# Head sums of two token groups moved from TensorE matmuls to a gather and VectorE additions, with the work around them re-ordered

## The chip, the cores and the metric

The kernel runs on one core of one Trainium2 chip. The metric is device time in microseconds (us). A run is compared with runs of the kernel before on the same chip. "PE" is TensorE's matmul side, "PEld" its weight loads, "DVE" VectorE, "ACT" ScalarE, "POOL" GpSimd, "SP" the engine that issues most loads.

## The reference, cut to what matters

Two layers; in each, dilated local attention (32 heads of 32, window of 8 positions with stride 2) and then a gelu feed-forward, each with layer norm and residual. S = 2048, D = 1024, F = 3584, bfloat16.

```python
x = A_x                                    # (1, 2048, 1024)
for _ in range(2):
    x = x + attention(layernorm(x))        # q, k, v = x @ wqkv; logits[s, w] = q[s] . k[s - 2w] * scale
                                           # masked where s - 2w < 0; softmax over w; values; @ wo
    x = x + gelu(layernorm(x) @ w1 + b1) @ w2 + b2
```

## The kernel before

Tokens go in groups of 512: groups 0 to 3 are the first layer, 4 to 7 the second. Per group: `gen_qkv` (192 full matmuls), `gen_wo` (the output projection, 64), `gen_ffn1` and `gen_ffn2` (224 each). The attention's products and sums are VectorE's, run beside the matmuls of other groups as "sides" of a stage. A group's softmax weights `a` are then spread, that is, copied by DMA to all partitions that need them (`abc`), and the products with V give the attention values `oT`, which the output projection reads. For a group's logits, products of Q and K chunks are added up over eight chunks (`new_prod`), and what is left must be summed over the four partitions of each head. Groups 2 and later do that by a DMA gather and three VectorE additions; groups 0 and 1 by matmuls with a 0/1 selector, in `head_sum`:

```python
def acc_tile():
    return psum.tile([P, T], F32, name="acc", bufs=6)          # six PSUM banks; "L" has the two others
...
def head_sum(n, last=True):
    ...
    for wh in range(2):
        for tb in range(NTT):                                  # four column tiles of the array
            mm(L[tb * H:(tb + 1) * H, wh * 4:(wh + 1) * 4, :], lhsT=smat[:],
               rhs=prod[:, tb, wh * 4:(wh + 1) * 4, :], start=start, ..., tile_position=(0, tb * H))
...
def ln_stats_ahead(g):                                         # group 3's statistics, on VectorE
    for tt in range(NTT):
        ln_stats(g * NTT + tt, mv_ahead[:, tt, :], rstd_ahead[:, tt, :])
...
# gen_qkv, group 0: four quarters of the weights as they land, on half the tokens
for kq in range(4 if n == 0 else 0):
    for c in range(6):
        first[c] = qkv_chunk(wq, c, xnT, first.get(c), kq * (KD // 4), (kq + 1) * (KD // 4), 0, 2)
        if (kq, c) in ((2, 5), (3, 5)):
            ...
            transpose_on_pe(*first_late.pop(0))                # tiles 2 and 3
...
# the main program
stage(q1, sides=at(6, attend, 0) + at(6, spread, 0) + at(6, hold) + each(new_prod, 1, 8, 1, 0, 4) + each(av, 0, 12, 1))
q2 = gen_qkv(2, defer=True)
stage(q2, 18)
new_prod(1, 4)
hold()
stage(gen_wo(0))                                               # reads oT, which av(0, c) writes
```

PSUM is the memory into which matmuls add up their results; each accumulation takes one bank of it. A bank of `acc` comes free when its reader has read it: for `gen_ffn2` and `gen_wo` that reader is VectorE. In the traces it takes its instructions one after the other in a fixed order, so such a read, here called a clear, can come late because other work stands ahead of it (4.4 us late in one place shown below).

## Time and profile before

| | before |
|---|---|
| median of the first 3 runs | 1233.41 us |
| span of the profiled run | 1230.8 us |
| PE busy, DVE busy | 99%, 70% |
| first real matmul; first of full width; last matmul | 8.92; 24.39; 1227.46 us |
| start to start of full matmuls | 0.216 us |

From the page of the kernel before, its part 1 (busy us, share of the span, instructions) and part 2 (granted TensorE clock in 40 slices):

```profile
PE 1222.2 (99%) x5739; PEld 632.6 (51%) x5789; DVE 861.9 (70%) x922; ACT 307.3 (25%) x491; POOL 87.2 (7%) x207
PEclk9999999999999999999999999999999999999999
```

From the list of waits of the kernel before, PE alone (engine, what it wanted, whom it waited for: total us, times, longest):

```profile
PE acc L219 <- DVE xn L93: 1.5, 1, 1.5
PE acc L118 <- DVE big L93: 1.1, 1, 1.1
PE acc L118 <- DMA wt<-in_A_wqkv_dram: 0.3, 1, 0.3
```

PE waits 2.9 us in all, and all of that lies before 12.1 us. Busy time alone would not show saturation, as matmuls overlap (one lasts 0.379 us in the trace); the starts do: after 24 us those of full matmuls are 0.216 us apart, but for a few longer steps around the two head sums (and steps of 0.43 us where the record of a matmul is missing). So only the two ends and whatever else PE has to do are to be gained.

Timeline of PE around the first head sum, kernel before (start us, us, engine, line, operation, output<-inputs, count):

```profile
62.80 1.46 PE L118 MATMUL acc<-xnT,wt 128*128 128x512 bf16 x6
64.19 0.61 PE L118 MATMUL L<-big,smat 128*32 128x512 bf16 x8
64.74 1.52 PE L118 MATMUL acc<-xnT,wt 128*128 128x512 bf16 x6
```

The eight selector matmuls start within 0.24 us (64.19 to 64.43), four at a time: four column tiles run side by side. From the first of them to the next full matmul it is 0.55 us.

Timeline of VectorE before the first output projection, and at the first clears of the first and second feed-forward, kernel before:

```profile
84.68 4.62 DVE L93 TENSOR_TENSOR big<-big 128x4096 bf16<-128x4096 bf16 x2
89.22 4.49 DVE L93 TENSOR_TENSOR big<-abc,vT 128x4096 bf16<-128x4096 bf16 x2
...
122.75 0.75 DVE L93 TENSOR_TENSOR oT<-big 128x512 bf16<-128x512 bf16 x2
...
222.19 0.67 DVE L93 TENSOR_TENSOR tmp<-acc,b2bc 128x512 f32<-128x512 f32 x1
...
371.65 0.69 DVE L93 TENSOR_TENSOR tmp<-acc,b2bc 128x512 f32<-128x512 f32 x1
```

Group 0's values begin at 89.22 us and end at 123.50; the projection starts at 125.23. The lines with `tmp<-acc` free PSUM banks.

### The profile page before, as it was taken

What the parts mean: (1) busy time and instruction counts of PE and PEld (TensorE: products, weight loads), DVE (VectorE), ACT (ScalarE), POOL (GpSimd) and SP (SyncE); (2) the same over time, 40 slices, a digit from 0 to 9 for tenths busy, and PEclk for the clock granted to TensorE, in tenths of its full rate; (3) what the DMA queues carried; (4) which work ended last, traced back from release to release, by engine and by line L of the source; (5) the groups of instructions that cost most, each with busy time, mean ns of one, the idle gap of its engine ahead of it and who ended that gap; (6) DMA issues with size and microseconds to landing.
All of it is one profiled execution on the core that took longest, in us unless ns stands there. A gap on an engine that the chain in (4) does not pass through costs nothing.

```text
span 1230.8 us, 13962 instructions
## 1 busy us (share of the span) xinstructions
PE 1222.2 (99%) x5739; PEld 632.6 (51%) x5789; DVE 861.9 (70%) x922; ACT 307.3 (25%) x491; POOL 87.2 (7%) x207
## 2 busy tenths in 40 slices
PE   9999999999999999999999999999999999999998
PEld 7666544456444564445544465444654444444444
DVE  7989899988998599375993759937599797011001
ACT  4343152014320143202431024310244101400310
POOL 3010010010010000100011000010000002000000
PEclk9999999999999999999999999999999999999999
DMA  9954665656556654856447565486664558446441
GB/s 290 300 179 143 182 222 185 201 154 209 181 165 215 180 162 163 229 172 186 150 163 238 171 171 170 158 223 202 171 196 145 188 196 208 151 158 196 155 135 52
DMA packets 219391, 225.06 MB, mean 183 GB/s; under 512 B 68194, under 2 KB 187136, under 8 KB 217024
## 3 DMA queue, kind: packets, MB, share of 16 engines
q1 hardware_dynamic: 214704, 208.69, 55.5%
q0 software_dynamic: 4624, 15.49, 3.3%
q8 instruction: 45, 0.74, 0.2%
q14 instruction: 18, 0.15, 0.0%
HBM read 191.11 MB, written 4.72 MB: 159 GB/s over the span
## 4 chain that ended last, share of the span: by engine, by line
PE 99%; DMA 1%; issue 0%; SPq 0%; DVE 0%
PE acc L118 98%; DMA wt<-in_A_wqkv_dram 1%; SPq L93 0%; PE L L118 0%; PE L L219 0%; DVE x L93 0%
## 5 line engine op out<-in xcount | busy, mean ns | idle before, releaser
L118 PE MATMUL acc<-xnT,wt 128*128 128x512 bf16 (+1 forms) x3392 | 720.9, 375 | 0.4 <-DMA wt<-in_A_wqkv_dram 0.3
L118 PEld LDWEIGHTS <-wt 128*128 128x128 bf16 x3392 | 400.5, 119 | 319.1 <-issue 1.4
L118 PE MATMUL acc<-wt,hT 128*128 128x512 bf16 (+1 forms) x1780 | 386.0, 376 | 2.1
L118 PEld LDWEIGHTS <-hT 128*128 128x128 bf16 x1820 | 178.1, 98 | 208.9
L93 DVE TENSOR_TENSOR big<-big 128x1024 bf16<-128x1024 bf16 (+2 forms) x184 | 245.2, 1360 | 2.2
L93 ACT ACTIVATE hT<-acc,b1T 128x512 bf16<-128x512 f32 x224 | 152.7, 688 | 332.3 <-PE acc L118 332.1
L93 DVE TENSOR_TENSOR big<-qT,kT 128x4096 bf16<-128x4096 bf16 x64 | 143.8, 2286 | 48.4 <-ACT kT L93 47.8
L93 DVE TENSOR_TENSOR big<-abc,vT 128x4096 bf16<-128x4096 bf16 x64 | 144.7, 2286 | 14.0 <-DMA abc<-a 13.4
L93 DVE TENSOR_TENSOR tmp<-acc,b2bc 128x512 f32<-128x512 f32 x56 | 38.6, 690 | 146.7 <-PE acc L118 143.7
L93 ACT CAST qT<-acc 128x512 bf16<-128x512 f32 (+1 forms) x72 | 38.0, 545 | 351.1 <-PE acc L118 351.1
L118 PE MATMUL acc<-wt,oT 128*128 128x512 bf16 x440 | 97.4, 379 | 0.4
L93 DVE BATCH_NORM_STATS2 stats<-x 128x6 f32<-128x512 bf16 x128 | 85.6, 682 | 4.5 <-DMA x<-in_A_x_dram 3.4
L118 PEld LDWEIGHTS <-oT 128*128 128x128 bf16 x448 | 43.8, 98 | 52.8
L93 DVE TENSOR_TENSOR x<-acc,big 128x512 bf16<-128x512 f32 (+1 forms) x9 | 5.7, 633 | 90.0 <-PE acc L118 90.0
L93 ACT CAST vT<-acc 128x512 bf16<-128x512 f32 x64 | 37.5, 586 | 83.3 <-PE acc L118 83.3
L93 ACT CAST kT<-acc 128x512 bf16<-128x512 f32 x64 | 37.4, 587 | 67.0 <-PE acc L118 67.0
L93 POOL TENSOR_TENSOR rstd<-mv,eps_t 128x1 f32<-128x1 f32 x56 | 14.2, 253 | 515.4 <-DVE mv L93 509.4
L93 DVE TENSOR_TENSOR x<-acc,x 128x512 bf16<-128x512 f32 x64 | 42.9, 671 | 4.8 <-PE acc L118 4.4
L93 DVE TENSOR_SCALAR xn<-x,mv,rstd 128x1024 bf16<-128x1024 bf16 x52 | 28.4, 547 | 20.2 <-POOL rstd L93 20.1
L93 DVE TENSOR_TENSOR x<-tmp,x 128x512 bf16<-128x512 f32 x56 | 38.7, 690 | 1.3
L93 POOL DMA_DIRECT2D big<-big x24 | 13.3, 565 | 256.3 <-DVE big L93 237.6
L93 POOL TENSOR_TENSOR rstd<-rstd,mhalf 128x1 f32<-128x1 f32 x56 | 31.0, 553 | 4.4
(68 smaller groups left out, 228.8 us busy)
## 6 DMA issues: line engine op xcount, KB each, us to landing
wt<-in_B_w_dram SPq DMA_DIRECT2D x56, 1024.0 KB, 5.7
wt<-in_B_w_dram SPq DMA_DIRECT2D x64, 896.0 KB, 4.9
wt<-in_A_wqkv_dram SPq DMA_DIRECT2D x46, 1024.0 KB, 5.6
wt<-in_A_wo_dram SPq DMA_DIRECT2D x16, 1024.0 KB, 5.0
big<-big POOLq DMA_DIRECT2D x24, 256.0 KB, 3.6
abc<-a POOLq DMA_DIRECT2D x24, 256.0 KB, 5.3
x<-in_A_x_dram SPq DMA_DIRECT2D x16, 256.0 KB, 6.2
out_dram<-x SPq DMA_DIRECT2D x31, 128.0 KB, 2.1
```

Of the source, the lines that this page charges most:

```text
L93: inst = f(*args, **kwargs)
L118: return pe(nc.tensor.matmul(*args, **kwargs))
```

## The change

Its intent: take the selector matmuls off PE, and make room on VectorE for what replaces them. Cut to its core:

```diff
-        return psum.tile([P, T], F32, name="acc", bufs=6)
+        return psum.tile([P, T], F32, name="acc", bufs=8)
...
-    def head_sum(n, last=True):  ...                      # gone; logits(n) sums a gather Lq for every group
+    def between(n, m):
+        vec.on = True                                     # VectorE in just this order
+        for c in range(3):
+            new_prod(m, c)
+        logits(n)
+        new_prod(m, 3, False)
+        weights(n)
+        spread(n)                                         # straight from SBUF; before: by way of DRAM
+        for _ in range(2):
+            add_prods(m)
+        vec.on = False
...
     def ln_stats_ahead(g):                                # group 3's statistics on ScalarE
+            act.activation(junk[:], x[t][:], ACT.Identity, scale=-1.0 / D, accum_out=less[:])
+            act.activation(junk[:], x[t][:], ACT.Square, bias=less[:], accum_out=var)
...
-            for c in range(6):
+            for c in range(7):
                 first[c] = qkv_chunk(...)
-                if (kq, c) in ((2, 5), (3, 5)):
+                if (kq, c) == (2, 3):  ...  transpose tile 2
+                if (kq, c) == (3, 4):  ...  transpose tile 3
...
-        hT = hpool.tile([P, KF, T], BF16, name="hT")
+        hT = [hpool.tile([P, KQ, T], BF16, name=f"hT{q}") for q in range(4)]
...
-        stage(q1, sides=at(6, attend, 0) + at(6, spread, 0) + at(6, hold) + each(new_prod, 1, 8, 1, 0, 4) + each(av, 0, 12, 1))
+        q1 = gen_qkv(1, defer=True, qk_pool=early, mix=NCH // 2)      # Q and K chunks take turns
+        stage(q1, sides=at(0, gather, 0) + at(11, between, 0, 1) + at(11, hold) + each(av, 0, 12, 1))
...
# group 2: products 4 to 7, its gather and softmax move from the first feed-forward
# to the V, Q and K chunks of group 3, after the second output projection
```

More of the change, by code (lines that the diff above doesn't have):

```diff
@@ L73 @@
     bigp = ctx.enter_context(tc.tile_pool(name="bigp", bufs=3))
-    dram = ctx.enter_context(tc.tile_pool(name="dram", bufs=2, space=bass.MemoryType.DRAM))
     smp = ctx.enter_context(tc.tile_pool(name="smp", bufs=1))
@@ L154 @@
     make_identity(nc, ident[:])
-    smat = const.tile([P, H], BF16, name="smat")
     mask = const.tile([P, W - 1, HALO], F32, name="mask")
@@ L166, in build_constants @@
         pool.memset(zhalo[:], 0.0)
-        pool.memset(smat[:], 1.0)
-        pool.affine_select(out=smat[:], in_=smat[:], pattern=[[-HP, H]], compare_op=ALU.is_ge, fill=0.0, base=0, channel_multiplier=1)
-        pool.affine_select(out=smat[:], in_=smat[:], pattern=[[HP, H]], compare_op=ALU.is_ge, fill=0.0, base=HP - 1, channel_multiplier=-1)
         pool.memset(mask[:], 0.0)
+        first = smp.tile([H, W - 1, HALO], F32, name="z")
+        pool.memset(first[:], 0.0)
         for w in range(W - 1):
-            pool.memset(mask[0:H, w, 0:HALO - DIL * w], -1e9)
-    def spread_mask():
-        first = smp.tile([H, W - 1, HALO], F32, name="mx")
-        vec.tensor_copy(first[:], mask[0:H, :, :])
-        vec.memset(mask[:], 0.0)
+            pool.memset(first[:, w, 0:HALO - DIL * w], -1e9)
         pool.dma_start(mask[0::NTT, :, :], first[:])
@@ L187, in transpose_bias @@
     def transpose_bias():
-        ps = psum.tile([P, KF], BF16, name="acc", bufs=6)
+        ps = psum.tile([P, KF], BF16, name="acc", bufs=8)
         pe(nc.tensor.transpose(ps[:], b1_rows[:], ident[:KF, :KF]))
@@ L205, in ln_stats_ahead @@
     def ln_stats_ahead(g):
+        junk = lnp.tile([P, D], BF16, name="xn", bufs=3)
         for tt in range(NTT):
-            ln_stats(g * NTT + tt, mv_ahead[:, tt, :], rstd_ahead[:, tt, :])
+            t, mean, var = g * NTT + tt, mv_ahead[:, tt, 0:1], mv_ahead[:, tt, 1:2]
+            less = lnp.tile([P, 1], F32, name="less")
+            act.activation(junk[:], x[t][:], ACT.Identity, scale=-1.0 / D, accum_out=less[:])
+            act.activation(junk[:], x[t][:], ACT.Square, bias=less[:], accum_out=var)
+            pool.tensor_scalar(out=mean, in0=less[:], scalar1=-1.0, scalar2=None, op0=ALU.mult)
+            rstd = rstd_ahead[:, tt, :]
+            pool.tensor_scalar(out=rstd, in0=var, scalar1=1.0 / D, scalar2=EPS, op0=ALU.mult, op1=ALU.add)
+            pool.tensor_tensor(out=rstd, in0=rstd, in1=mhalf[:], op=ALU.pow)
     def ln_norm(t, mv, rstd, xn=None):
@@ L213, in ln_norm, with transpose_on_pe @@
         return xn
-    def transpose_on_pe(xn, out, pst=None, parts=None):
-        if pst is None:
-            pst = psum.tile([P, KD, P], BF16, name="acc", bufs=6)
+    def transpose_on_pe(xn, out, parts=None):
+        pst = psum.tile([P, KD, P], BF16, name="acc", bufs=8)
         for k in range(KD):
@@ L237, in ln_first @@
         vec.on = act.on = True
-        both = psum.tile([P, 2, KD, P], BF16, name="L", bufs=1)
         mvs = {}
@@ L267, in ln_first @@
         for tt in range(2, 4):
-            first_late.append((norm(tt), xa[0][:, tt, :, :], both[:, tt - 2, :, :]))
+            first_late.append((norm(tt), xa[0][:, tt, :, :]))
         vec.on = act.on = False
@@ L290, in qkv_chunk, with add_prods, new_prod @@
         return ps
-    def head_sum(n, last=True):
-        if "L" not in st[n]:
-            st[n]["L"] = psum.tile([P, W, P], F32, name="L", bufs=1)
-            start = True
-        else:
-            start = False
-        L = st[n]["L"]
-        prod = st[n]["prods"].pop(0)
-        for wh in range(2):
-            for tb in range(NTT):
-                mm(L[tb * H:(tb + 1) * H, wh * 4:(wh + 1) * 4, :], lhsT=smat[:],
-                   rhs=prod[:, tb, wh * 4:(wh + 1) * 4, :], start=start,
-                   stop=last, skip_group_check=True, tile_position=(0, tb * H))
-    def new_prod(n, c):
+    def add_prods(n):
+        tree = st[n]["prods"]
+        b = tree.pop()
+        vec.tensor_tensor(out=tree[-1][:], in0=tree[-1][:], in1=b[:], op=ALU.add)
+    def new_prod(n, c, add=True):
         s = st[n]
@@ L312, in new_prod, with gen_qkv @@
         vec.tensor_tensor(out=prod[:], in0=q.unsqueeze(2).to_broadcast([P, NTT, W, P]), in1=win_by_tile(s["kT"][:, c, :]), op=ALU.mult)
-        tree = s["prods"]
-        tree.append(prod)
-        if c % 2 == 1:
-            for _ in range(1 if c % (NCH // s["parts"]) == 1 else 2):
-                b = tree.pop()
-                vec.tensor_tensor(out=tree[-1][:], in0=tree[-1][:], in1=b[:], op=ALU.add)
-    def gen_qkv(n, parts=1, defer=False, qk_pool=None, v_late=False, qk_next=None):
+        s["prods"].append(prod)
+        if add and c % 2 == 1:
+            for _ in range(1 if c == 1 else 2):
+                add_prods(n)
+    def gen_qkv(n, defer=False, qk_pool=None, v_late=False, qk_next=None, v_first=False, mix=0):
         g = n % NG
@@ L323, in gen_qkv, with values @@
         s = st[n]
-        s["parts"] = parts
         s["prods"] = []
         qk_pool = qk_pool or attp
+        if v_first:
+            wv = load_qkv(2)
         wq = wq_first if n == 0 else load_qkv(0)
-        wk = load_qkv(1)
+        if not v_first:
+            wk = load_qkv(1)
+        def values():
+            vT = attp.tile([P, NCH, HALO + T], BF16, name="vT", bufs=2)
+            s["vT"] = vT
+            act.on = n > 2
+            act.copy(vT[:, :, 0:HALO], (zhalo if g == 0 else vhalo)[:])
+            act.on = False
+            for c in range(NCH):
+                ps = qkv_chunk(wv, c, xnT)
+                act.copy(vT[:, c, HALO:], ps[:])
+                yield
+            if g + 1 < NG:
+                act.copy(vhalo[:], vT[:, :, T:T + HALO])
+        if v_first:
+            yield from values()
+            wk = load_qkv(1)
         if n == 0:
@@ L339, in gen_qkv @@
         for kq in range(4 if n == 0 else 0):
-            for c in range(6):
+            for c in range(7):
                 first[c] = qkv_chunk(wq, c, xnT, first.get(c), kq * (KD // 4), (kq + 1) * (KD // 4), 0, 2)
-                if (kq, c) in ((2, 5), (3, 5)):
-                    for done in range(2 if kq == 3 else 0):
+                if (kq, c) == (2, 3):
+                    transpose_on_pe(*first_late.pop(0))
+                if (kq, c) == (3, 4):
+                    for done in range(2):
                         act.copy(qT[:, done, 0:2 * P], first[done][:, 0:2 * P])
                     transpose_on_pe(*first_late.pop(0))
+                    act.hold()
+        if n == 0:
+            first[7] = qkv_chunk(wq, 7, xnT, t0=0, t1=2)
         for c in list(first)[2:]:
             act.copy(qT[:, c, 0:2 * P], first[c][:, 0:2 * P])
-        for c in range(6 if n == 0 else NCH, NCH):
-            ps = qkv_chunk(wq, c, xnT, t0=0, t1=2)
-            act.copy(qT[:, c, 0:2 * P], ps[:, 0:2 * P])
-        for c in range(NCH):
-            t0 = 2 if n == 0 else 0
-            ps = qkv_chunk(wq, c, xnT, t0=t0)
-            act.copy(qT[:, c, t0 * P:], ps[:, t0 * P:])
-            yield
-        if n > 0 and not v_late:
-            wv = load_qkv(2)
         kT = qk_pool.tile([P, NCH, HALO + T], BF16, name="kT")
@@ L362, in gen_qkv, with query, key @@
         act.on = False
-        for c in range(NCH):
+        def query(c):
+            t0 = 2 if n == 0 else 0
+            ps = qkv_chunk(wq, c, xnT, t0=t0)
+            act.copy(qT[:, c, t0 * P:], ps[:, t0 * P:])
+        def key(c):
             ps = qkv_chunk(wk, c, xnT)
@@ L367, in gen_qkv @@
                 new_prod(n, c)
+        ahead = mix or NCH
+        turns = [(query, c) for c in range(ahead)]
+        for c in range(NCH):
+            turns.append((key, c))
+            if ahead + c < NCH:
+                turns.append((query, ahead + c))
+        for i, (chunk, c) in enumerate(turns):
+            if i == NCH and n > 0 and not v_late and not v_first:
+                wv = load_qkv(2)
+            chunk(c)
             yield
@@ L370, in gen_qkv @@
             act.copy(khalo[:], kT[:, :, T:T + HALO])
-        vT = attp.tile([P, NCH, HALO + T], BF16, name="vT", bufs=2)
-        s["vT"] = vT
-        if v_late:
-            wv = load_qkv(2)
-        act.on = n > 2
-        act.copy(vT[:, :, 0:HALO], (zhalo if g == 0 else vhalo)[:])
-        act.on = False
-        for c in range(NCH):
-            ps = qkv_chunk(wv, c, xnT)
-            act.copy(vT[:, c, HALO:], ps[:])
-            yield
-        if g + 1 < NG:
-            act.copy(vhalo[:], vT[:, :, T:T + HALO])
+        if not v_first:
+            if v_late:
+                wv = load_qkv(2)
+            yield from values()
     def gather(n):
@@ L388, in gather @@
         prod = s["prods"].pop(0)
-        Lq = bigp.tile([P, HP, W, P], BF16, name="big")
+        Lq = attp.tile([P, HP, W, P], BF16, name="abc") if n < 2 else bigp.tile([P, HP, W, P], BF16, name="big")
         s["Lq"] = Lq
@@ L400, in fold, with logits, weights @@
         return t[:, 0, :]
-    def attend(n):
+    def logits(n):
         s = st[n]
+        Lq = s.pop("Lq")
         e = smp.tile([P, W, P], F32, name="e")
-        if "Lq" in s:
-            Lq = s.pop("Lq")
-            vec.tensor_tensor(out=e[:], in0=Lq[:, 0, :, :], in1=Lq[:, 1, :, :], op=ALU.add)
-            for j in range(2, HP):
-                vec.tensor_tensor(out=e[:], in0=e[:], in1=Lq[:, j, :, :], op=ALU.add)
-            L = e
-        else:
-            head_sum(n)
-            L = s.pop("L")
-        if n % NG == 0:
-            p = H if n == 0 else P
-            vec.tensor_tensor(out=L[0:p, 0:W - 1, 0:HALO], in0=L[0:p, 0:W - 1, 0:HALO], in1=mask[0:p, :, :], op=ALU.add)
-        if n < 2:
-            mx = smp.tile([P, P], F32, name="mx")
-            vec.tensor_reduce(out=mx[:], in_=L[:].rearrange("p w t -> p t w"), axis=AX.X, op=ALU.max)
-            mx = mx[:]
-        else:
-            mx = fold(L, ALU.max)
-        vec.tensor_tensor(out=e[:], in0=L[:], in1=mx.unsqueeze(1).to_broadcast([P, W, P]), op=ALU.subtract)
+        vec.tensor_tensor(out=e[:], in0=Lq[:, 0, :, :], in1=Lq[:, 1, :, :], op=ALU.add)
+        for j in range(2, HP):
+            vec.tensor_tensor(out=e[:], in0=e[:], in1=Lq[:, j, :, :], op=ALU.add)
+        if n % NG == 0:
+            vec.tensor_tensor(out=e[:, 0:W - 1, 0:HALO], in0=e[:, 0:W - 1, 0:HALO], in1=mask[:], op=ALU.add)
+        mx = fold(e, ALU.max)
+        vec.tensor_tensor(out=e[:], in0=e[:], in1=mx.unsqueeze(1).to_broadcast([P, W, P]), op=ALU.subtract)
+        s["e"] = e
+    def weights(n):
+        s = st[n]
+        e = s.pop("e")
         act.on = 1 < n < N - 1
@@ L432, in attend @@
         s["a"] = a
+    def attend(n):
+        logits(n)
[4 more added lines that the diff above has]
+            new_prod(m, c)
+        logits(n)
+        new_prod(m, 3, False)
+        weights(n)
+        spread(n)
+        for _ in range(2):
+            add_prods(m)
+        vec.on = False
     def spread(n):
@@ L440, in spread @@
         s["oT"] = attp.tile([P, NCH, T], BF16, name="qT" if n == N - 1 else "oT")
-        if n < 2:
-            a_d = dram.tile([H, NTT, W, P], BF16, name="a_d")
-            for tb in range(NTT):
-                pool.dma_start(a_d[:, tb, :, :], a[tb * H:(tb + 1) * H, :, :])
-            a = a_d
         for j in range(HP):
@@ L494, in gen_ffn1 @@
                     mm(ps[:], lhsT=wt[:, k, jj * P:(jj + 1) * P], rhs=xnT[:, :, k, :], start=(k == 0), stop=(k == KD - 1))
-                act.activation(hT[:, j, :], ps[:], ACT.Gelu_apprx_tanh, bias=b1T[:, j:j + 1])
+                act.activation(hT[j // KQ][:, j % KQ, :], ps[:], ACT.Gelu_apprx_tanh, bias=b1T[:, j:j + 1])
                 yield
@@ L520, in gen_ffn2 @@
                         for k in range(KQ):
-                            mm(ps, lhsT=hT[:, kq * KQ + k, tt * P:(tt + 1) * P], rhs=wt[:, k, cs],
+                            mm(ps, lhsT=hT[kq][:, k, tt * P:(tt + 1) * P], rhs=wt[:, k, cs],
                                start=(kq == 0 and k == 0), stop=(kq == 3 and k == KQ - 1))
@@ L596 @@
         stage(gen_qkv(0, qk_next=early), sides=at(14, load_b2))
-        q1 = gen_qkv(1, defer=True, qk_pool=early)
-        stage(q1, sides=at(6, attend, 0) + at(6, spread, 0) + at(6, hold) + each(new_prod, 1, 8, 1, 0, 4) + each(av, 0, 12, 1))
+        q1 = gen_qkv(1, defer=True, qk_pool=early, mix=NCH // 2)
+        stage(q1, sides=at(0, gather, 0) + at(11, between, 0, 1) + at(11, hold) + each(av, 0, 12, 1))
         q2 = gen_qkv(2, defer=True)
         stage(q2, 18)
-        new_prod(1, 4)
         hold()
@@ L604 @@
         hold()
-        stage(q2, sides=each(new_prod, 1, 0, 1, 5, 8))
+        stage(q2, sides=each(new_prod, 1, 0, 1, 4, 8))
+        gather(1)
     hpool = ctx.enter_context(tc.tile_pool(name="hpool", bufs=1))
-    stage(gen_ffn1(0), sides=at(5, attend, 1) + at(5, spread, 1) + at(5, hold) + each(new_prod, 2, 2, 1)
-          + at(10, gather, 2) + at(10, hold) + each(av, 1, 10, 2, 0, 4))
+    stage(gen_ffn1(0), sides=each(new_prod, 2, 2, 1, 0, 3) + at(5, hold) + at(5, attend, 1) + at(5, spread, 1) + at(5, hold) + at(6, new_prod, 2, 3)
+          + at(10, hold) + each(av, 1, 10, 2, 0, 4))
     stage(gen_ffn2(0), sides=at(0, ln_stats_ahead, 3) + at(15, hold) + at(15, ln_a, 3, None, True) + each(av, 1, 16, 1, 4, 8) + at(23, hold))
     for n in range(1, N - 2):
-        stage(gen_wo(n), sides=at(0, spread, n + 1) if n > 1 else at(7, hold) + at(7, attend, 2))
-        stage(gen_qkv(n + 2), sides=(at(0, spread, 2) if n == 1 else []) + each(av, n + 1, 0, 2, 0, 3))
-        if n == 1:
-            spread_mask()
+        early_av = 3 if n > 1 else 0
+        stage(gen_wo(n), sides=(at(0, spread, n + 1) if n > 1 else []) + (at(7, hold) if n < 3 else []))
+        stage(gen_qkv(n + 2, v_first=n == 1), sides=each(av, n + 1, 0, 2, 0, early_av) if n > 1 else
+              each(new_prod, 2, 0, 1, 4, 8) + at(3, gather, 2) + at(10, hold) + at(10, logits, 2) + at(19, weights, 2) + at(19, spread, 2))
         gather(n + 2)
-        stage(gen_ffn1(n), sides=(at(20, attend, n + 2) if n + 3 == N else []) + each(av, n + 1, 8, 2, 3, 8))
+        stage(gen_ffn1(n), sides=(at(20, attend, n + 2) if n + 3 == N else []) + each(av, n + 1, 8 - 2 * (3 - early_av), 2, early_av, 8))
         if n + 3 < N:
```

## The prediction

> **What bounds it now.** TensorE. The page has PE busy 99% of 1230.8 us, clock 1.00, and the list of waits gives PE only 2.9 us of waiting, all before 12.1 us. Busy time alone would prove little (the Trainium skill, "Trainium Kernel Development and Optimization", Performance Expectations, calls it a bad metric because matmuls are pipelined), so I read start-to-start times in the timeline: 0.216 us for each 128x512 matmul from 24 us to the end; the 0.43 us steps are missing records. This agrees with "TensorE: Matmul & The Clock Gate", Part 1 (215.7 ns warm). The 5,632 full-width-equivalent matmuls need 5632 x 0.2158 = 1215.4 us, untouched by the change. Only about 15 us can be gained at all, mostly start (first real matmul at 8.92 us) and tail. VectorE is 70% busy, but 99% in 30 to 124 us.
>
> **What the change removes from PE.** Two head sums of 8 selector matmuls, at 64.2 and 159.9 us. From the last matmul before to the first after is 0.86 us, less its own 0.216: 0.64 us each, because the four column tiles overlap. Total 1.28 us. At the start, seven chunks instead of six per quarter give PE 0.44 us more work before the third weight piece, where it now stands 0.49 us; but the copy of tile 3's transpose then comes nearly due, so I count 0.35 us.
>
> **What it adds.** Group 0 and 1 logits go through a gather (about 5.4 us from first issue to last landing in group 2, hidden behind three products) and three VectorE additions (1.22 us each), 3.7 us a group, plus 0.2 us for fold instead of reduce. Layer statistics leave VectorE for ScalarE (6 us less in the first feed-forward stage), four products of group 2 move behind the second output projection: both relieve VectorE before 247 us, and use idle VectorE afterwards (over 20 us idle from 260 to 400 us). Quartered gelu buffer and eight PSUM buffers: PE did not wait there, so nothing.
>
> **The critical place.** Attention values of group 0 must be ready for the first output projection. Before: chain of VectorE from 29.7 us, values start 89.22, end 123.50; projection starts 125.23, its eighth matmul (which reads the last chunk) 126.7: slack 3.2 us. After: PE arrives about 1.0 us earlier (125.75 for that matmul). VectorE: 63.75 + three products and an addition 9.1 + logits 6.75 + product 2.3 + weights 3.65 = 85.7 (up to 0.5 more if exp is late); direct spread needs about 5.8 us as in group 2 (8.5 in group 3), so values start about 91.5, end about 125.9. I expect PE to wait 0 to 0.6 us there, perhaps 2 us if the spread meets weight loads. Later projections keep slack.
>
> **Sum.** 1233.4 - 1.28 - 0.35 + 0.3 = 1232.1 us. Range 1231.0 to 1234.5. Faster by over 2%: 1%; within 2%: 97%; slower by over 2%: 2%.
>
> **What would show it.** No selector matmuls, no 0.86 us steps; first full-width matmul at about 24.0 us instead of 24.39; VectorE waiting about 1 us for the spread near 90 us; PE in the list of waits with at most about 1 us for group 0's values near 125 us; all other steps still 0.216 us; VectorE busy time 4 to 6 us different, without effect.
>
> **What would make it wrong.** A slow spread or late exp makes the wait at 125 us 2 to 4 us; a static ScalarE or VectorE order that holds back PSUM evictions; the start losing more on the tile 3 transpose, which now shares the PSUM pool; group 2's later logits delaying the third projection.

## The result and the profile after

The changed kernel takes 1231.15 us (median of 6; 1230.84 to 1231.43) against 1233.31 us (median of 6; 1232.55 to 1233.82): ratio 0.9983, 95% interval 0.997 to 0.9996. The spans of the two profiled runs are 1229.1 and 1230.8 us. A gain is there, of 0.17%: far within 2%.

Part 1 of the page and the granted clock, kernel after:

```profile
PE 1221.3 (99%) x5723; PEld 632.7 (51%) x5773; DVE 864.2 (70%) x918; ACT 315.1 (26%) x507; POOL 105.2 (9%) x209
PEclk9999999999999999999999999999999999999999
```

PE alone and PEld alone in the list of waits, kernel after, the lines that matter:

```profile
PE acc L218 <- DVE xn L92: 1.1, 1, 1.1
PE acc L117 <- DVE big L92: 1.0, 1, 1.0
...
PEld L117 <- DVE oT L92: 0.3, 1, 0.3
```

The wait for the weights at the start is gone; one new wait, of 0.3 us, is put down to group 0's attention values (`oT`).

Timeline of PE where the head sum was, kernel after: one unbroken group.

```profile
61.64 5.56 PE L117 MATMUL acc<-xnT,wt 128*128 128x512 bf16 x25
```

Timeline of VectorE at the places shown of before, kernel after (in brackets the idle time before the line and what ended it):

```profile
84.06 4.61 DVE L92 TENSOR_TENSOR big<-big 128x4096 bf16<-128x4096 bf16 x2
90.65 4.50 DVE L92 TENSOR_TENSOR big<-abc,vT 128x4096 bf16<-128x4096 bf16 x2 [1.98 <-DMA abc<-a]
...
124.19 0.75 DVE L92 TENSOR_TENSOR oT<-big 128x512 bf16<-128x512 bf16 x2
...
216.57 0.69 DVE L92 TENSOR_TENSOR tmp<-acc,b2bc 128x512 f32<-128x512 f32 x1 [12.36 <-PE acc L117]
...
381.41 0.68 DVE L92 TENSOR_TENSOR tmp<-acc,b2bc 128x512 f32<-128x512 f32 x1
```

Three things are to be seen. The values end at 124.94 us, 1.4 us later than before, while PE comes about 1.2 us earlier. In the first feed-forward VectorE now waits for PE (12.36 us idle) instead of coming 4.4 us late. In the second it comes at 381.41 us for an accumulation that was ready at 368.1 us: 13.3 us late, where it had been 1.9 us late.

Where the time came from, by matmul starts in the traces ("first" is the first real matmul, "full" the first of full width, "last" the last one; all 14 traces):

```
                                    first    full-first   last-full   last-first
before                              8.919    15.468       1203.070    1218.538
after                               8.953    14.915       1201.915    1216.830
after, again (e11)                  9.039    14.914       1201.719    1216.633
e1 selectors five times             9.424    14.915       1207.357    1222.272
e2 gather of group 1 alone          8.976    15.140       1210.053    1225.193
e3 before, values later             8.901    15.211       1208.575    1223.786
e4 after, values later              8.872    14.917       1207.772    1222.689
e5 after, old start                 8.904    15.392       1201.719    1217.111
e6 after, projection later          9.116    14.912       1201.719    1216.631
e7 after, stats on VectorE, one hT  8.797    15.036       1201.719    1216.755
e8 after, ffn weights later         8.790    14.914       1202.969    1217.883
e9 after, old start, six banks      8.947    15.416       1210.044    1225.460
e10 e2 with stats on ScalarE        8.852    15.172       1204.957    1220.129
e12 e6 again                        8.981    14.917       1201.719    1216.636
```

Between before and the repeat of after, the middle loses 1203.070 - 1201.719 = 1.351 us, or 0.68 us for each of the two head sums, and the start 0.55 us. Five traces have the very same 1201.719 us: there PE has no wait left after the start. The first real matmul moves by 0.6 us over these traces, even between traces of the same kernel (8.95 and 9.04; 9.12 and 8.98); it waits for the first rows of x. That is one reason that the spans and the runs differ by less or more than the 1.7 to 1.9 us found here.

### The profile page after: what moved, and what is told of

Read it like the earlier page. It is cut to its first block, busy times and chain, and to the rows that moved or that the text cites. A ratio compares the mean times of both kernels' runs of the same rounds, so it can differ in the third digit from the quotient of the medians.

```text
span 1229.1 us, 13953 instructions
## 1 busy us (share of the span) xinstructions
PE 1221.3 (99%) x5723; PEld 632.7 (51%) x5773; DVE 864.2 (70%) x918; ACT 315.1 (26%) x507; POOL 105.2 (9%) x209
## 4 chain that ended last, share of the span: by engine, by line
PE 99%; DVE 0%; issue 0%; DMA 0%
PE acc L117 99%; DMA x<-in_A_x_dram 0%; DVE stats L92 0%; PE acc L218 0%; DVE xn L92 0%; DVE x L92 0%; DVE mv L92 0%; PE acc L181 0%; DVE rstd L92 0%
## 5 line engine op out<-in xcount | busy, mean ns | idle before, releaser
L92 DVE BATCH_NORM_STATS2 stats<-x 128x6 f32<-128x512 bf16 x120 | 79.9, 680 | 3.7 <-DMA x<-in_A_x_dram 2.7
L92 POOL TENSOR_TENSOR rstd<-mv,eps_t 128x1 f32<-128x1 f32 x56 | 17.4, 311 | 527.5 <-DVE mv L92 527.5
L92 POOL DMA_DIRECT2D big<-big x24 | 13.3, 563 | 212.8 <-DVE big L92 212.8
```

The costliest lines, as they stand in the source:

```text
L92: inst = f(*args, **kwargs)
```

## The experiments

All twelve gave correct results. e1 to e4 ran in one set of 3 rounds, e5 to e8 and e9 to e12 in sets of 5; the time of before given with each is that of the same set.

### e1: the selectors five times over (on the kernel before)

```diff
-        for wh in range(2):
+        for wh in [w for _ in range(5) for w in range(2)]:
```

> The kernel before, with the eight selector matmuls of each of its two head sums done five times over (each time from a fresh start, so the result stays right). Theory A (TensorE is the bound, a selector costs its array time in full): each of the 2 x 4 extra passes costs about 0.43 us (8 matmuls of 512 columns, four column tiles side by side), 3.5 us in all; the trace shows the two selector places grown from 0.86 us to about 2.6 us and everything after shifted by that. Rival B (the selectors hide under waits that PE has anyway): 0 to 0.5 us.

Measured: 1237.05 us against 1233.12, ratio 1.003 (1.0015 to 1.0045). Timeline of PE at the first head sum:

```profile
61.68 2.54 PE L118 MATMUL acc<-xnT,wt 128*128 128x512 bf16 x11
64.14 2.34 PE L118 MATMUL L<-big,smat 128*32 128x512 bf16 x40
66.42 2.81 PE L118 MATMUL acc<-xnT,wt 128*128 128x512 bf16 x12
```

From the last matmul before to the first after is 66.42 - 63.84 = 2.58 us, where it was 0.86 us: 0.43 us for each of four further passes, as theory A said. 0.43 us is two full matmul times for eight matmuls. The rest of a head sum's 0.68 us, about 0.25 us, is entering and leaving. The Trainium skill, "TensorEngine Tiling (Array Packing)", Tiling Modes, Key Properties, says that changing the tiling mode drains TensorE; this trace fits, with steps of 0.31, 0.31 and 0.27 us around the selectors in place of 0.216. Another 0.8 us of waits in this run are at the first two output projections. At the first it is a load: the second half of the weights landed at 128.12 us for a matmul due at 127.78. The wait at the second is put down to attention values; I did not follow it further.

### e2: group 1 through the gather, alone (on the kernel before)

```diff
-        if n < 2:
+        if n < 1:
             a_d = dram.tile(...)
...
         stage(q2, sides=each(new_prod, 1, 0, 1, 5, 8))
+        gather(1)
```

> The kernel before, with group 1 alone moved from selector matmuls to the gather and three VectorE additions; nothing of what the change moves off VectorE. Theory A (PE's sum alone decides): 0.70 us less. Rival B (VectorE's chain to the second output projection is within about 1.2 us of PE in the kernel before, and gets 3.9 us longer): the 0.70 us is lost again and PE waits about 2 to 2.5 us for group 1's attention values near 246 us, so the kernel is 1 to 2 us longer than before.

Measured: 1239.40 us against 1233.12, ratio 1.005 (1.0033 to 1.0067). The sign of rival B was right, the place and the size were not. The one wait of size in PE's list, and VectorE's timeline at the first clear of the first feed-forward:

```profile
PE acc L118 <- DVE tmp L93: 5.4, 1, 5.4
```

```profile
229.89 0.67 DVE L93 TENSOR_TENSOR tmp<-acc,b2bc 128x512 f32<-128x512 f32 x1
```

PE waits not for attention values but for a PSUM bank. VectorE's extra work (additions 3.7 us, 2.94 us idle for the gather, a maximum that takes 1.90 us instead of 1.22) stands ahead of the clears, which start at 229.89 us instead of 222.19. With six banks, the second half of the feed-forward has four accumulations to open and two free banks, so the third must wait for the first clear. In the kernel before it was due at 222.57 (start of the second half) + 14 x 0.216 = 225.6 us, and the clear was done at 222.9: 2.7 us to spare. Here it was due at 225.07 us, and the clear was done at 229.89 + 0.67 = 230.56. Another 1.5 us follows, because seven matmuls after the wait run 0.427 us apart: the granted clock is 0.50 for 3.41 us in this trace's clock record.

### e3 and e4: group 0's values later, before and after

The same three unused VectorE products ahead of the values, in both kernels:

```diff
+    def late(n, c, count):                      # count products into a tile that nothing reads, in order
...
-  ... + each(av, 0, 12, 1)
+  ... + at(11, late, 1, 3, 3) + each(av, 0, 12, 1)
```

> The kernel before, with three unused VectorE products (2.28 us each, 6.8 us) put ahead of group 0's attention values. Theory A (VectorE's chain has 3.0 us of slack to the first output projection): PE waits there about 3.8 us, and the kernel is 3.8 us longer. Rival B (VectorE is off the critical path): no change.

> The same three unused products in the changed kernel, at the same place. Theory A (the slack there is now 2.0 us of waiting for the spread plus about 0.3 us): PE waits about 4.4 us and the kernel is about 4.4 us longer than the changed one (some 2.3 us longer than before). Rival B (VectorE is off the critical path): no change against the changed kernel.

Measured: e3 1237.62 us and e4 1237.73 us against 1233.12 (both ratios 1.0036, 1.0021 to 1.0051). PE's timeline at the projection, e4:

```profile
123.94 1.46 PE L117 MATMUL acc<-wt,oT 128*128 128x512 bf16 x5
129.49 4.77 PE L117 MATMUL acc<-wt,oT 128*128 128x512 bf16 x13 [4.09 <-DVE oT L92]
```

Counted over the 0.216 us step, PE stands 4.3 us in e4 and 3.3 us in e3, with some tenths after. The three products push the values back by 6.6 us, so the slack was about 3.3 us before (3.0 expected) and is about 2.3 us after (2.3 expected): VectorE's chain is tied to the critical path in both kernels, and rival B is out. Both expectations of the whole time are too short all the same. By the traces, e3 is 5.5 us longer than before from the first full-width matmul to the last (3.8 expected), of which 0.5 us is a wait for weights at 24.8 us that has nothing to do with the edit; e4 is 5.9 us longer than the changed kernel (4.4 expected). The rest is the clock: seven matmuls after each wait run 0.427 us apart instead of 0.216, which is 1.5 to 1.7 us that I had left out of the sum.

### e5: the old start (on the kernel after)

```diff
-            for c in range(7):
+            for c in range(6):
...
-                if (kq, c) == (2, 3):
+                if (kq, c) == (2, 5):
-                if (kq, c) == (3, 4):
+                if (kq, c) == (3, 5):
```

> The changed kernel with the start of before: six Q chunks instead of seven per quarter, tiles 2 and 3 transposed after the third and fourth quarter. Theory A (the seventh chunk fills the wait for the third weight piece): 0.5 us longer than the changed kernel, first full-width matmul at 24.4 us instead of 23.87, a wait of about 0.5 us near 11.5 us. Rival B (the start is given by when the first rows arrive, and the chunk count is free): within 0.1 us.

Measured: 1230.99 us against 1232.60, ratio 0.9986 (0.9973 to 0.9998): whole runs don't tell it from the changed kernel. The trace does: 15.392 us from first to full-width matmul instead of 14.914, and a step of 0.42 us beyond the usual at 11.45 us. Over all traces, the seven with the old start average 15.25 us (14.92 to 15.47), the seven with the new one 14.93 us: 0.31 us. The wait that the seventh chunk fills depends on when that load lands, and sometimes there is none (e1).

### e6 and e12: the first projection one V chunk later (on the kernel after)

```diff
-        stage(q2, 18)
+        stage(q2, 19)
```

> The changed kernel with the first output projection one V chunk (1.73 us) later. Both theories of the 0.20 us wait at 124.9 us (A: second half of the projection's weights lands late; B: group 0's last attention values) give no wait there: 0.2 us shorter than the changed kernel, if the one chunk less behind the projection is still enough to hide its layer norm and transposes; if it isn't, a new wait at the first feed-forward matmul.

Measured: 1230.81 us against 1232.60, ratio 0.9985 (0.9972 to 0.9997). No wait after the start; 1216.631 us from first to last matmul against 1216.830 in the first trace of the changed kernel. It was run again beside the changed kernel itself:

> The version with the first output projection one V chunk later once more, on the same chip and in the same rounds as the changed kernel: from the first real matmul to the last again 1216.6 us, no wait of PE after the start; at most 0.2 us shorter than the changed kernel, which whole runs will hardly resolve.

> The changed kernel once more, to see what changes from trace to trace without any edit. If the 0.20 us wait for the projection's second weight half is a matter of that one load, it comes and goes; the first real matmul moves by up to 0.3 us with the load of the first rows; from the first real matmul to the last, the time is 1216.6 to 1216.9 us.

Measured: e12 1231.05 us and e11, the changed kernel, 1230.78 us, against 1232.81 (ratios 0.9987 and 0.9986). From first to last matmul 1216.636 and 1216.633 us: equal. So there is nothing to be gained by this edit that the unedited kernel doesn't also have when its 0.20 us wait happens not to occur.

### e8: the feed-forward's first weights later (on the kernel after)

```diff
-            if n == 0 and j4 == 1:
+            if n == 0 and j4 <= 1:
                 dep_order(load, last_transpose[0], "transposes first")
```

> The changed kernel with one queue order changed: the first feed-forward weight load comes behind the transposes of the first projection, so that it no longer shares the DMA engines with the second half of the projection's weights. VectorE as before. Theory A (the 0.20 us wait at 124.9 us is for those weights, which land at 125.03 us): they land about 1 to 2.5 us sooner and the wait is gone, 0.2 us less. Rival B (the wait is for group 0's attention values, as the list of waits names VectorE): the wait stays.

Measured: 1232.16 us against 1232.60, ratio 0.9996 (0.9984 to 1.0009): a miss as a version, since the load is now too late for its own reader. PE in the list of waits of e8:

```profile
PE acc L117 <- DMA wt<-in_B_w_dram: 1.1, 1, 1.1
```

The 0.20 us wait is gone, but that alone doesn't decide, as it is gone in e7 and e11 too. What decides is the landing of the load, read from the semaphore's updates. In the trace of the changed kernel, the second half of the projection's weights lands at 125.03 us and the matmul that asks for it, due at 124.88, starts at 125.08; the values had to be there only for the weight load of the eighth chunk, near 125.3 us, and were there at 124.95. In e11 the load lands at 124.89 for a matmul at 124.96, in e7 at 124.79 for 124.84, in e8 at 124.53 for 124.71. So the wait was for a load that lands within 0.2 us of its need, and the list of waits named the wrong engine. In e8 the load landed 0.5 us sooner, not the 1 to 2.5 us expected.

### e7: statistics back on VectorE, gelu buffer in one piece (on the kernel after)

```diff
-            act.activation(junk[:], x[t][:], ACT.Identity, ...)   # and what follows
+            ln_stats(g * NTT + tt, mv_ahead[:, tt, :], rstd_ahead[:, tt, :])
...
-        hT = [hpool.tile([P, KQ, T], BF16, name=f"hT{q}") for q in range(4)]
+        hT = hpool.tile([P, KF, T], BF16, name="hT")
```

> The changed kernel with two parts undone that I count as free: group 3's layer statistics back on VectorE (about 6 us of its time), and the gelu buffer in one piece. Theory A (VectorE ends group 1's values 3.5 us before the second projection starts, plus 1.5 us until they are read; PE never waited for the gelu buffer): within 0.3 us of the changed kernel, PE waits under 0.3 us near 245 us. Rival B (these parts carry the gain): 1 us or more longer.

Measured: 1231.43 us against 1232.60, ratio 0.9992 (0.9978 to 1.0006), and in the trace 1201.719 us from full-width to last matmul, no wait near 245 us. The two parts, undone together, are free: in this schedule they gain nothing.

### e9: the old start, and six banks instead of eight (on the kernel after)

```diff
-        return psum.tile([P, T], F32, name="acc", bufs=8)
+        return psum.tile([P, T], F32, name="acc", bufs=6)
...
+        both = psum.tile([P, 2, KD, P], BF16, name="L", bufs=1)   # the two late transposes, as before
```

> The changed kernel with the old start (as in the old-start run) and also the old share of PSUM: six banks for accumulators, two apart that only the two late transposes use. Theory A (with group 2's products moved behind the second projection, VectorE clears the banks in time, so two more banks gain nothing): within 0.3 us of the old-start run, no PE wait over 0.3 us after 30 us. Rival B (the two further banks carry the gain): PE waits for banks, in the first feed-forward's second half near 222 us above all, and it is 1 us or more longer.

Measured: 1239.63 us against 1232.81, ratio 1.0058 (1.0045 to 1.007). Beside e5 the trace is 1210.044 - 1201.719 = 8.3 us longer. Of that, 0.7 us is no wait for a bank: at 25.0 us PE stands for a weight load that lands at 25.83 us (in the second line of the list; e2 and e3, with the old start too, have the same wait, shorter). The other 7.6 us are one wait for a bank and its aftermath. My theory A falls, and the place of rival B was wrong as well: PE waits in the second feed-forward, not in the first. PE in the list of waits, and the timelines of PE and of VectorE there:

```profile
PE acc L117 <- DVE tmp L92: 5.9, 1, 5.9
...
PE acc L117 <- DMA wt<-in_A_wqkv_dram: 0.8, 2, 0.5
```

```profile
373.64 3.40 PE L117 MATMUL acc<-wt,hT 128*128 128x512 bf16 x15
382.91 3.47 PE L117 MATMUL acc<-wt,hT 128*128 128x512 bf16 x8 [5.88 <-DVE tmp L92]
```

```profile
382.18 0.68 DVE L92 TENSOR_TENSOR tmp<-acc,b2bc 128x512 f32<-128x512 f32 x1
```

VectorE clears at 382.18 us here and at 381.41 us in the changed kernel: equally late, 13 us after the accumulation is ready. With six banks PE stops at the third accumulation of the second half until that clear is done at 382.86 us; with eight it opens all four and never notices. Counted over the usual step PE stands 6.0 us, and eight matmuls then run at half the clock (8 in 3.47 us), 1.6 us more. So the two banks that the head sum's output had held are what keeps the moved work off the critical path.

### e10: e2 with the statistics on ScalarE (on the kernel before)

> The kernel before with group 1 through the gather, as in the gather-alone run, and with the changed kernel's layer statistics on ScalarE. Theory A (the gather-alone run lost because VectorE cleared the first feed-forward's PSUM banks 7.7 us later, where 2.7 us were free): taking 6.3 us off VectorE ahead of those clears gives them back in time, the 5.55 us wait near 225 us falls below 0.5 us, and what is left is at most about 1.5 us of wait for group 1's values at the second projection, so the kernel is between 0.7 us shorter and 1 us longer than before. Rival B (something else of the gather, such as its DMA, costs the 6 us): it stays 5 us or more longer than before.

The edit is that of e2, with the `ln_stats_ahead` of the change. Measured: 1233.96 us against 1232.81, ratio 1.001 (0.9997 to 1.0023). The wait near 225 us is 0.50 us instead of 5.55, and a wait of 1.43 us for group 1's values comes at 247.8 us, as theory A said; the total is 1.15 us over before, just outside the range that I had given. With six banks and group 2's products in their old place, moving the statistics is worth 5 us; e7 shows that with eight banks and the products moved it is worth nothing.

## Why the prediction was right or wrong

Predicted 1232.1 us (1231.0 to 1234.5), measured 1231.15: inside, at the low end; the class "within 2%" was right too. Point by point:

- **PE is the bound and its 0.216 us steps are untouched.** Right: 1201.719 us of unbroken matmuls in five traces.
- **Selectors cost 0.64 us each, 1.28 us in all.** Right: 1.35 us by the traces, and e1 shows that PE pays for each further pass in full.
- **0.35 us at the start.** Right on average: 0.31 us over seven against seven traces, 0.55 us between the first trace of before and either of after. It is a wait for a load, so it varies from trace to trace.
- **The critical place is the first projection; values start about 91.5 and end about 125.9 us; PE waits 0 to 0.6 us.** The mechanism was right (e3, e4), with the values 0.9 us sooner than that (90.65 and 124.94). The exponential cost VectorE no wait at all, and the spread took 6.5 us from the end of `a` to the first product that reads it. So the 0.3 us put in the sum for this wait was an overestimate: the trace with a wait had 0.20 us, and that one was for weights. The list of waits showed "DVE oT", just as I had said it would, and was wrong.
- **"They relieve VectorE before 247 us, and use idle VectorE afterwards."** The first half was right. The second was half the story: it comes 13.3 us late in the second feed-forward.
- **"Quartered gelu buffer and eight PSUM buffers: PE did not wait there, so nothing."** This is the step that failed. For the gelu buffer it holds (e7). For the banks it doesn't: that PE did not wait for banks in the kernel before says nothing of a schedule that delays their clears. Taking the two banks back costs 7.6 us (e9, without its wait for weights at the start), about four times the whole gain. It did not show in the predicted time because the change brings both, the lateness and the banks. That the number held in spite of this step was luck: the prediction had not weighed the one against the other.
- **What would make it wrong.** "A static VectorE order that holds back PSUM evictions" was on the list, and it is what e2, e9 and, at 0.5 us, e10 ran into; I had not connected it with the bank count. VectorE's busy time differs by 2.3 us, not by 4 to 6.

The Trainium skill points at the banks: "PSUM — Partial Sum Buffer", Specifications, gives eight of them per partition, and "Perfetto Trace Analysis", Matmul Optimizations, advises to use all eight. e9 puts a price on it in this kernel.

What stays open: which of the moves of group 2's work is needed beside the banks. Only the whole of it was run, and the first feed-forward with the old place of the products and eight banks was not tried. The whole runs show a gain of 2.0 to 2.2 us and the traces 1.7 to 1.9; with an interval from 0.04% to 0.3% that is no contradiction, and the moving start of the first matmul is larger than the difference.

## What to carry to other kernels

When a saturated engine gets rid of a small helper operation, cost not only the time of the operation (here 0.68 us each) but the buffers that it frees: two PSUM banks were worth more than the matmuls. A buffer for which nobody waits is free only in the schedule that was profiled; before moving work ahead of an in-order engine's clears, compute when the next accumulation needs a bank, from the number of banks, and compare it with when the clear will be done. And when effects are below the scatter of whole runs, compare start times of the bottleneck's instructions from a common anchor, over several traces; a wait of some tenths may be one load's luck, and the engine named beside it may not be the one.

## What the Trainium skill lacked or had wrong

- "TensorE: Matmul & The Clock Gate", Part 1: it says that the clock falls to half after an idle window of about 3.4 us and comes back after about as long a busy one. The length of the window agrees: with waits of 3.3, 4.3 and 5.5 us (e3, e4, e2) the clock record has 0.50 for 3.413 us each time, with 6.0 us (e9) for twice that, 6.827 us; after 1.43 us (e10) it stays at 1.00. That a whole window has to be idle does not: in e9 the record falls at 379.33 us, only 2.3 us after the modelled end of the last matmul before the wait (377.04). A single such wait cost 1.5 to 1.7 us on top, in seven or eight matmuls at 0.427 instead of 0.216 us, in e2, e3, e4 and e9 alike. The page's own rule for this price (Terms: throttled time times one half) gives 3.4 us for e9, an estimate, where 1.6 us was measured. It would have to count only the throttled time after the wait: 3.24 us in e9 (382.91 to 386.15), of which half is 1.6 us.
- "TensorEngine Tiling (Array Packing)", Tiling Modes: it says that a change of mode drains TensorE, without a figure. Here entering and leaving the four-column mode cost about 0.25 us together, and eight 128x32 selectors in it 0.43 us, the time of two full matmuls.
- "Perfetto Trace Analysis", Matmul Optimizations: the advice to use all eight banks has no measure of when it pays. Here six banks were enough with a clear 4.4 us late (2.7 us to spare), and cost 6.0 us of waiting with one 13 us late.
- No page that I read has the jitter of a load's landing near its need: the same 1 MB weight load landed 0.05 to 0.18 us before its matmul was due (e7, e11, e8) or 0.16 us after (the first trace of the changed kernel).
